# Three chunks per bank instead of two in the second MLP's output projection of tokens 256 to 1279, second half first, and output weights decoded a chunk later

## The chip, the cores and the metric

The kernel runs on one core of a Trainium2 chip. The metric is the device time of one execution in microseconds (us). Engines: PE multiplies matrices (PEld is its weight load, which overlaps), DVE is the vector engine, ACT the scalar engine, POOL the general-purpose engine, SP issues most DMAs.

## The reference

`attn_out` is an attention over a window of 64 positions (4 sequences of 576 tokens, 8 heads of 64). Its output is 2304 tokens by 512 features and goes through two gated MLPs with d_ff = 1536:

```python
def _moe_ref(x, w_gate, w_val, w_out):
    gate = 1.0 / (1.0 + np.exp(-(x @ w_gate)))
    return (gate * (x @ w_val)) @ w_out

def _moe2_ref(x, w_a, w_b, w_out):
    return ((x @ w_a) * (x @ w_b)) @ w_out

x = _moe_ref(attn_out as 2304 x 512, first weights)
return _moe2_ref(x, second weights)
```

The change touches the second MLP alone.

## The kernel before

**Chunks and split products.** d_ff is cut into 12 chunks of 128 columns. Each fp32 operand is a pair, a high and a low part in PE's own fp32 format, and each product is three matmuls (high by high, high by low, low by high). In the names, `wh`/`wl`, `xh`/`xl`, `hh`/`hl` are such parts.

**Weights.** The weights come as 64-bit words and are decoded on chip, matrix by matrix: a, b and o (the output matrix) of a chunk. For one matrix, `decode_words` (line 371) issues ACT L374 and L377, DVE L380 and L383, POOL L387; `decode_pair` (line 392) issues DVE L393, ACT L399 (the high part) and L402 (the low part, on DVE for a and b, on POOL for o), and `save` stores the pair to DRAM for later stages. Raw words arrive through three staging buffers `st`; when decoding of a matrix begins, the load of the same matrix of the next chunk is issued (`load_matrix`). The order of decoding is the list `order` (line 637): a, b, o of a chunk, then of the next. `step_decode` takes one step of it, `need(F)` takes steps until chunk F is `ready`. Decoded pairs lie in the pool `wts`, four buffers for each of a, b and o. F counts the chunks of both MLPs, so second-MLP chunk fc is F = 12 + fc. POOL and ACT also form sums of the chunk's a and b for the products below (`wq`, lines 439 to 442, called combinations here).

**The stage.** The change is in the stage that works on tokens 256 to 1279 with the second MLP, 343.6 to 592.25 us of the trace. These four blocks go through the first two products together, as a scheme of seven products per chunk (`quad`, matmuls at L846, in the order 1, 5, 6, 2, 7, 4, 3). PSUM results are kept or added by ACT L865 and DVE L868, DVE L878 multiplies a by b, and the result is two halves: h0, ready within the chunk, from pool `hp` (5 buffers for each part), and h1, ready at its end, in one of three places taken in turn (`seconds`: a buffer of its own, one of `wts` tag wa, one of tag wb). L470 writes a high part `hh`.

**The output projection.** `row_banks` (L1103) lists eight jobs for h0 and h1 of two chunks (PAIR = 2): four row blocks of h0, then four of h1. A job is `bank_sum` (L980): its matmuls (L984), three for each chunk, run into one PSUM bank `accq` (pool `ps_acc`, two buffers); then ACT L986 copies the bank to the sum `resf` (first pair), or DVE L988 adds it (all later ones). The jobs wait in a list `rest`; `fill(n)` issues n of them. `between(i)`, called after product i of a quad, issues some (a table `counts`) and takes one step of decoding. After each second quad what is left of `rest` is issued and the next eight jobs are listed.

**Block 0.** Tokens 0 to 255 are taken along: before quads 0, 2 and 4, `hidden` (L461 matmuls, L485, L470) computes two chunks of block 0 each ("the alone chunks"), and their projection (L514, added at L584 and L586) is one more job in `rest`.

**What sets the order.** A scheduler moves instructions within each engine's queue, so the order of the code is not the order on the engine; the excerpts in the section on the change show the orders that result. Each engine runs its own queue strictly in that order.

**What comes behind.** The last bank sums of this stage run beside `hidden` of chunks 9 to 11 of block 0; then the same seven products begin for another set of tokens, at 592.25 us.

Of the kernel before, what the change touches and what calls it, by code (L numbers as in the profile page):

```python
# [21 lines left out]
def tile_window_attention_gated_mlps(ctx, tc, q, k, v, w1g, w1v, w1o, w2a, w2b, w2o, out):  # L22
# [5 lines left out]
    NP = H // 2  # L28
    NF = DFF // P
    G = 3  # L30
    N = 256
# [337 lines left out]
    def decode_words(F, i, nm):  # L369
        st = staged.pop((F, nm))  # L370
        w0, w1 = st[:, :, 0], st[:, :, 1]
        k = 3 * F + i if F > NF + 2 else 0
        low = dec.tile([P, DM], I32, tag="low", name="low")
        nc.scalar.activation(out=low, in_=w0.bitcast(U32), func=AF.Copy, scale=2.0 ** -29)  # L374
        yield
        ex = late["dec"].tile([P, DM], F32, tag="ex", name="ex") if k % 3 == 2 else dec.tile([P, DM], F32, tag="ex", bufs=2, name="ex")
        nc.scalar.activation(out=ex, in_=w1.bitcast(F32), func=AF.Abs)  # L377
        yield
        wi = (late["dec"] if k % 2 else dec).tile([P, DM], I32, tag="wi", name="wi")
        nc.vector.tensor_scalar(  # L380
            out=wi, in0=w1, scalar1=3, scalar2=(1 << 30) - 1, op0=ALU.logical_shift_left, op1=ALU.bitwise_and
        )
        nc.vector.scalar_tensor_tensor(  # L383
            out=wi, in0=w1, scalar=-(1 << 30), in1=wi, op0=ALU.bitwise_and, op1=ALU.bitwise_or
        )
        yield
        nc.gpsimd.tensor_tensor(out=wi, in0=wi, in1=low, op=ALU.add)  # L387
        wordy[F, nm] = ex, wi
        yield
# [244 lines left out]
    NW = 2 * NF  # L634

    limit = [NF - 1]
    order = [(F, i, nm) for F in range(DECODED, NW) for i, nm in enumerate("abo")]
    held = [None]
    begun, pending, combined_by = [0], [], []

    def begin_matrix():
        if begun[0] == 0:
            load_weights(DECODED)
        if begun[0] < len(order):
            F, i, nm = m = order[begun[0]]
            begun[0] += 1
            since = len(nc.cur_bb.bb.instructions)
# [7 lines left out]
            pending.append(m)  # L655
            if F + 1 < NW:
                load_matrix(F + 1, nm)

    def step_decode(turn):
# [16 lines left out]
        save(F, nm, pairs.pop((F, nm)))  # L676
        if nm == "o":
            ready[F] = parts[F]
        elif nm == "b" and F >= NF:
            combined_by.append(combining(F))  # L680
        return True

# [7 lines left out]

    def need(F, turn):
        while F not in ready:
            assert step_decode(turn), (F, turn)
# [408 lines left out]

    def row_banks(res, hs, rows, begin, end):  # L1103


        banks = []
        for i in range(2 * NP):
            j, sl = i // NP, slice(i % NP * P, (i % NP + 1) * P)
# [17 lines left out]
    x_ops = next(built)  # L1126
    PAIR = 2
    NEVER = 1 << 30
# [10 lines left out]
    for fc in range(NF):  # L1139
        alone = ALONE.get(fc, ())  # L1140
        for i, f0 in enumerate(alone):
# [4 lines left out]
            if i == len(alone) - 1:  # L1146
                rest.append(lambda a=(1, 0, h0s, fc == 0, False): projection(*a))
                h0s = []
# [7 lines left out]
        g = [tmp.tile([P, W], F32, tag="hr", name=f"g{i}") for i in range(2)]  # L1156
        counts = ((0, 0, 1, 1, 1, 1, 0), (0, 0, 1, 1, 1, 1, 0)) if len(rest) <= 4 else ((0, 1, 1, 1, 1, 1, 1), (0, 1, 1, 1, 1, 1, 1))
        extra = max(0, len(rest) - sum(counts[0]))

        def between(i):  # L1160
            fill(counts[0][i] + (extra if i == 4 else 0))
            if i != 3:
                step_decode(NEVER)

        hs.append((w["o"], quad(1, w, x_ops, between, g, seconds[fc % 3], lambda: None)))
        if len(hs) == PAIR:
            fill(len(rest))
            row_banks(res, hs, (3 * N, N), fc == PAIR - 1, fc == NF - 1)
            hs = []
# [10 lines left out]
    h0s = []  # L1180
# [147 lines left out]
```

## Time and profile before

| | us |
|---|---|
| time, median of three runs | 965.94 |
| lowest and highest run | 965.51, 966.07 |
| profiled execution, its own time | 966.96 |
| span in that profile | 965.1 |
| PE busy | 927.0 (96%) |
| DVE busy | 705.4 (73%) |
| ACT busy | 480.0 (50%) |
| POOL busy | 358.7 (37%) |

The span runs from the first to the last instruction on the engines; 1.9 us of the profiled execution's time lie around it. PE is close to full over the whole span, so what can be gained or lost by another order of the same matmuls is PE's idle time, which has to be looked for stage by stage: a window's length less PE's busy time in it. In a timeline, the bracket behind an instruction names the idle time ahead of it and what ended it. The granted clock of PE is 1.00 in every window of the stage.

### The profile page before, as it was taken

To read this page: it belongs to the slowest core of one execution; us is meant where nothing else is said; L and a number is where in the kernel's file an instruction comes from. 1 tells how busy PE (TensorE), PEld (TensorE's weight loads), DVE (VectorE), ACT (ScalarE), POOL (GpSimd) and SP (SyncE) were. 2 spreads that over 40 slices of the span, in tenths; PEclk is the share of its full clock that TensorE was granted. 3 is DMA by queue.
4 is the path that set the end of the run, shared out by engine and by line. 5 is a ranking of instruction groups with operands and counts; after the bars stand their busy time and mean duration, and the time that the engine had idled before them with its cause. 6 is when DMAs were issued, how large, how long until landed. Compare 5 with 4: busy or idle time off the path is not lost.

```text
span 965.1 us, 15642 instructions
## 1 busy us (share of the span) xinstructions
PE 927.0 (96%) x5504; PEld 772.7 (80%) x5504; DVE 705.4 (73%) x1343; ACT 480.0 (50%) x1063; POOL 358.7 (37%) x357
## 2 busy tenths in 40 slices
PE   7899999999999988899999998999999999999998
PEld 6798888888887766787777886788888888888886
DVE  7997877876567899967979576778888673354545
ACT  7887555677635456564645334654454233211111
POOL 4443232343248738855758217644440000000000
PEclk9999999999999999999999999999999999999999
DMA  8987698997478637763765547345456675554312
GB/s 213 247 238 222 217 316 287 336 292 239 138 235 287 218 131 233 257 210 130 251 231 195 196 151 254 117 160 168 135 173 199 217 254 159 167 168 129 102 66 87
DMA packets 144684, 193.68 MB, mean 201 GB/s; under 512 B 63584, under 2 KB 98912, under 8 KB 143968
## 3 DMA queue, kind: packets, MB, share of 16 engines
q1 hardware_dynamic: 144608, 192.71, 61.6%
q8 instruction: 43, 0.70, 0.3%
q14 instruction: 33, 0.27, 0.1%
HBM read 118.75 MB, written 69.47 MB: 195 GB/s over the span
## 4 chain that ended last, share of the span: by engine, by line
PE 48%; DVE 9%; POOL 3%; DMA 3%; issue 2%; ACT 1%; DVEq 0%; POOLq 0%; ACTq 0%
PE qa L846 16%; PE accq L984 11%; PE qb L846 8%; PE qc L846 4%; PE accy L947 3%; PE accx L947 2%; DVE wi L380 1%; DMA st_a<-in_moe_w_a_dram 1%; DVE ex L393 1%; POOL s L439 1%; DVE wi L383 1%; POOL wq L442 1%; PE gps L461 1%; PE vps L461 1%; PE acc L514 1%
## 5 line engine op out<-in xcount | busy, mean ns | idle before, releaser
L387 POOL TENSOR_TENSOR wi<-wi,low 128x512 int32<-128x512 int32 x72 | 103.9, 1443 | 144.2 <-DVE wi L383 109.6
L865 ACT ACTIVATE r<-qa 128x512 f32<-128x512 f32 x108 | 63.6, 596 | 107.6 <-PE qa L846 93.6
L442 POOL TENSOR_TENSOR wq<-s,wq 128x256 fp32r<-128x256 f32 x96 | 86.5, 907 | 73.7 <-ACT wq L441 72.3
L846 PE MATMUL qa<-op,wq 128*128 128x512 f32 x432 | 112.9, 389 | 0.4 <-ACT r L865 0.4
L846 PE MATMUL qb<-op,wq 128*128 128x512 f32 x432 | 111.1, 389 | 0.9 <-DVE qc L868 0.9
L461 PE MATMUL gps<-xh,wa 128*128 128x256 f32 (+1 forms) x392 | 104.9, 338 | 1.5 <-DVE h L472 1.0
L461 PE MATMUL vps<-xh,wb 128*128 128x256 f32 (+1 forms) x392 | 105.3, 337 | 0.8 <-ACT hr L485 0.8
L846 PEld LDWEIGHTS qb<-op,wq 128*128 128x128 f32 x432 | 81.0, 188 | 18.1 <-DVE qc L868 1.3
L846 PEld LDWEIGHTS qa<-op,wq 128*128 128x128 f32 x432 | 80.9, 188 | 17.3 <-ACT r L865 0.6
L562 PE MATMUL accm<-hh,wo 128*128 128x512 f32 (+1 forms) x296 | 87.3, 362 | 3.3 <-DVE gacc L539 1.9
L461 PEld LDWEIGHTS gps<-xh,wa 128*128 128x128 f32 x392 | 68.6, 189 | 11.4 <-DVE h L472 1.5
L461 PEld LDWEIGHTS vps<-xh,wb 128*128 128x128 f32 x392 | 68.9, 189 | 8.7 <-ACT hr L485 1.0
L984 PE MATMUL accq<-wo,h 128*128 128x512 f32 (+1 forms) x300 | 71.7, 382 | 2.8 <-DVE resf L988 2.7
L393 DVE SCALAR_TENSOR_TENSOR ex<-ex,wi 128x512 f32<-128x512 f32 x72 | 59.7, 829 | 17.7 <-POOL wi L387 10.3
L984 PEld LDWEIGHTS accq<-wo,h 128*128 128x128 f32 x300 | 54.9, 188 | 14.9 <-DVE resf L988 3.8
L461 PE MATMUL gps<-xl,wa 128*128 128x256 f32 (+1 forms) x196 | 65.6, 335 | 0.6 <-DVE xl L237 0.6
L470 ACT ACTIVATE hh<-qa 128x512 fp32r<-128x512 f32 x36 | 21.6, 599 | 89.0 <-DVE qa L878 60.0
L461 PE MATMUL vps<-xl,wb 128*128 128x256 f32 (+1 forms) x196 | 65.6, 335 | 0.0
L562 PEld LDWEIGHTS accm<-hh,wo 128*128 128x128 f32 x296 | 54.1, 193 | 13.8 <-DVE gacc L539 4.4
L984 PE MATMUL accq<-wo,hh 128*128 128x512 f32 x184 | 55.7, 394 | 4.9 <-ACT hh L470 3.7
L846 PE MATMUL qa<-op,wa 128*128 128x512 f32 x216 | 55.7, 391 | 3.3 <-DVE g L868 3.3
L846 PE MATMUL qa<-op,wb 128*128 128x512 f32 x216 | 55.3, 391 | 2.4 <-ACT r L865 2.4
(177 smaller groups left out, 2114.9 us busy)
## 6 DMA issues: line engine op xcount, KB each, us to landing
wo<-ko SPq DMA_DIRECT2D x27, 512.0 KB, 3.9
wa<-ka SPq DMA_DIRECT2D x27, 512.0 KB, 4.6
st_o<-in_moe_w_out_dram SPq DMA_DIRECT2D x24, 512.0 KB, 4.9
ka<-wa SPq DMA_DIRECT2D x24, 512.0 KB, 5.1
kb<-wb SPq DMA_DIRECT2D x24, 512.0 KB, 4.1
ko<-wo SPq DMA_DIRECT2D x24, 512.0 KB, 4.0
kq<-wq SPq DMA_DIRECT2D x48, 256.0 KB, 3.2
wq<-kq SPq DMA_DIRECT2D x48, 256.0 KB, 3.2
```

Of the source, the lines that this page charges most:

```text
L380: nc.vector.tensor_scalar(out=wi, in0=w1, scalar1=3, scalar2=(1 << 30) - 1, op0=ALU.logical_shift_left, op1=ALU.bitwise_and)
L383: nc.vector.scalar_tensor_tensor(out=wi, in0=w1, scalar=-(1 << 30), in1=wi, op0=ALU.bitwise_and, op1=ALU.bitwise_or)
L387: nc.gpsimd.tensor_tensor(out=wi, in0=wi, in1=low, op=ALU.add)
L393: nc.vector.scalar_tensor_tensor(out=wf, in0=wf, scalar=SMALLEST, in1=wi.bitcast(F32), op0=ALU.is_ge, op1=ALU.mult)
L442: nc.gpsimd.tensor_tensor(out=t[:, 1], in0=s, in1=t[:, 0].bitcast(F32), op=ALU.subtract)
L461: nc.tensor.matmul(ps, lhsT=a[:, c * P:(c + 1) * P], rhs=b[:, c, :], start=(n == 0), stop=(n == 3 * NP - 1))
L470: nc.scalar.activation(out=hh, in_=hr, func=AF.Copy, scale=factor)
L562: nc.tensor.matmul(ps[:, m], lhsT=a[:, sl], rhs=b, start=k == 0, stop=k == total - 1)
L846: nc.tensor.matmul(ps, lhsT=a[:, c * P:(c + 1) * P], rhs=b[:, c, :], start=first and n == 0, stop=n == 5, skip_group_check=True,)
L865: nc.scalar.activation(out=r[n], in_=ps, func=AF.Copy)
L947: nc.tensor.matmul(bank[k], lhsT=a[n][i][:, sl], rhs=b[n][j], start=start and m == 0, stop=m == 2, skip_group_check=True,)
L984: nc.tensor.matmul(ps, lhsT=a, rhs=b, start=n == 0, stop=n == len(pairs) - 1)
```

## The change

**Banks over three chunks.** `THREE = 3` takes the place of `PAIR`: eight jobs are listed after quads 2, 5, 8 and 11, each of nine matmuls instead of six. That is 32 jobs in place of 48 (the very last one is split in two by columns, as before). The number of matmuls is the same. In the first three quads there is no bank sum to issue; before, there was none in the first two.

**Second half first.** `turned=True` lists the four h1 jobs ahead of the four h0 jobs.

**Order of decoding.** Above F = 14, `order` has a and b of a chunk ahead of o of the chunk before; o of the last chunk comes last. A chunk is ready when its b is there and its combinations are formed; `need(..., "o")` stands ahead of a projection and of a list of banks. Loads follow `order`, three matrices ahead, and the buffers `ex` and `wi` are chosen by the place in `order`.

**Issue.** `counts` becomes (0, 1, 1, 0, 1, 1, 0) for every quad, four jobs; what four a quad don't take of `rest` (`extra`) is issued in the third quad after a list, behind product 4.

Everything else is the same, line numbers of the changed kernel apart (L846 is L851 there, L868 L873, L878 L883, L984 L989, L986 L991, L988 L993, L755 L760, L758 L763).

```diff
 def decode_words(F, i, nm):
-        k = 3 * F + i if F > NF + 2 else 0
+        k = order.index((F, i, nm)) if F > NF + 2 else 0
...
-    order = [(F, i, nm) for F in range(DECODED, NW) for i, nm in enumerate("abo")]
+    order = [(F, i, nm) for F in range(DECODED, NF + 2) for i, nm in enumerate("abo")]
+    for F in range(NF + 2, NW):
+        order += [(F, 0, "a"), (F, 1, "b")] + ([(F - 1, 2, "o")] if F > NF + 2 else [])
+    order.append((NW - 1, 2, "o"))
...
-            if F + 1 < NW:
-                load_matrix(F + 1, nm)
+            if at + 3 < len(order):
+                load_matrix(*order[at + 3][::2])
...
-        if nm == "o":
+        if nm == "o" and F < NF:
             ready[F] = parts[F]
         elif nm == "b" and F >= NF:
             combined_by.append(combining(F))
+            ready[F] = parts[F]
...
-    def need(F, turn):
-        while F not in ready:
+    def need(F, turn, nm="b"):
+        while F not in ready or nm not in parts[F] or nm == "b" and combined_by:
...
-    def row_banks(res, hs, rows, begin, end):
+    def row_banks(res, hs, rows, begin, end, turned=False):
-        for i in range(2 * NP):
+        for i in (*range(NP, 2 * NP), *range(NP)) if turned else range(2 * NP):
...
-                rest.append(lambda a=(1, 0, h0s, fc == 0, False): projection(*a))
+                def projected(a=(1, 0, h0s, fc == 0, False), last=NF + f0):
+                    need(last, NEVER, "o")
+                    projection(*a)
+
+                rest.append(projected)
...
-        counts = ((0, 0, 1, 1, 1, 1, 0), (0, 0, 1, 1, 1, 1, 0)) if len(rest) <= 4 else ((0, 1, 1, 1, 1, 1, 1), (0, 1, 1, 1, 1, 1, 1))
-        extra = max(0, len(rest) - sum(counts[0]))
+        counts = (0, 1, 1, 0, 1, 1, 0)
+        extra = max(0, len(rest) - sum(counts)) if len(hs) == THREE - 1 else 0
...
-        if len(hs) == PAIR:
+        if len(hs) == THREE:
             fill(len(rest))
-            row_banks(res, hs, (3 * N, N), fc == PAIR - 1, fc == NF - 1)
+            need(NF + fc, NEVER, "o")
+            row_banks(res, [(w["o"], h) for w, h in hs], (3 * N, N), fc == THREE - 1, fc == NF - 1, True)
```

PE's queue in quads 1 and 2, before. `qa`, `qb`, `qc` are PSUM banks of the seven products, `op` and `wq` their token and weight operands, `x6` six matmuls in a row:

```order
L846 MATMUL qa_4995<-op7_4762,wq7_4421 128x512 x6
L846 MATMUL qc_5229<-op2_4617,wa_4866 128x512 x6
L846 MATMUL qa_4995<-op4_4766,wb_4370 128x512 x6
L846 MATMUL qb_4996<-op3_4768,wq3_4427 128x512 x6
L846 MATMUL qa_5227<-op6_4725,wq6_4924 128x512 x6
L984 MATMUL accq_5160<-wo_4442,hh_5097 128x512 x2
L984 MATMUL accq_5168<-wo_4442,hh_5097 128x512 x2
```

The same place in the changed kernel:

```order
L851 MATMUL qa_4980<-op7_4762,wq7_4380 128x512 x6
L851 MATMUL qc_5182<-op2_4616,wa_4866 128x512 x6
L851 MATMUL qa_4980<-op4_4766,wb_4362 128x512 x6
L851 MATMUL qb_4981<-op3_4768,wq3_4386 128x512 x6
L851 MATMUL qa_5180<-op6_4725,wq6_4924 128x512 x6
L461 MATMUL gps_5112<-xh1_0_4728,wa_4866 128x256
```

The bank sums of the first pair, which stood here, are gone from this place; the alone chunks' `hidden` comes next.

DVE's queue at the start of the stage, before (`ex`, `wi`: decoding; `xl1`, `op4`: token operands):

```order
L393 SCALAR_TENSOR_TENSOR ex_4857<-ex_4857,wi_4859 128x512
L571 TENSOR_TENSOR xl1_0_4729<-gacc0_1020,xh1_0_4728 128x512 x2
L380 TENSOR_SCALAR wi_4880<-st_o_4439 128x512
L755 TENSOR_TENSOR op4_4766<-gacc30_2076,op4_4766 128x1024
L402 TENSOR_TENSOR wb_4887<-ex_4857,wb_4887 128x512
L383 SCALAR_TENSOR_TENSOR wi_4880<-st_o_4439,wi_4880 128x512
```

And in the changed kernel:

```order
L393 SCALAR_TENSOR_TENSOR ex_4857<-ex_4857,wi_4859 128x512
L571 TENSOR_TENSOR xl1_0_4729<-gacc0_1020,xh1_0_4728 128x512 x2
L393 SCALAR_TENSOR_TENSOR ex_4895<-ex_4895,wi_4897 128x512
L380 TENSOR_SCALAR wi_4995<-st_b_4446 128x512
L760 TENSOR_TENSOR op4_4766<-gacc30_2076,op4_4766 128x1024
L402 TENSOR_TENSOR wb_4904<-ex_4857,wb_4904 128x512
L383 SCALAR_TENSOR_TENSOR wi_4995<-st_b_4446,wi_4995 128x512
```

The o matrix that was decoded here (`st_o`) has given its place to the next chunk's b (`st_b`), with its L393 a step earlier.

ACT's queue where the first list of banks ends, before:

```order
L377 ACTIVATE ex_5517<-st_a_5389 128x512
L986 ACTIVATE resf3_4841<-accq_5317 128x512
L377 ACTIVATE ex_5654<-st_b_5428 128x512
L399 ACTIVATE wo_5392<-ex_5269 128x512
L986 ACTIVATE resf3_4841<-accq_5334 128x512
L399 ACTIVATE wa_5663<-ex_5517 128x512
L377 ACTIVATE ex_5443<-st_o_5275 128x512
```

And in the changed kernel:

```order
L470 ACTIVATE hh_5535<-vps_5519 128x256
L485 ACTIVATE hr_5587<-gps_5561 128x256
L991 ACTIVATE resf1_4839<-accq_5594 128x512
L470 ACTIVATE hh_5590<-vps_5574 128x256
L399 ACTIVATE wo_5491<-ex_5375 128x512
L399 ACTIVATE wo_5700<-ex_5652 128x512
L991 ACTIVATE resf1_4839<-accq_5605 128x512
L377 ACTIVATE ex_5781<-st_b_5637 128x512
```

Two o matrices (`wo_5491`, `wo_5700`) and an `hh` of the alone chunks now stand between the copies of the list's last two banks (`accq_5594`, `accq_5605`), ahead of the further decoding.

## Rows read from the trace of the kernel before

**Rows 1.** The page, busy time of each engine over the whole span

```profile
PE 927.0 (96%) x5504; PEld 772.7 (80%) x5504; DVE 705.4 (73%) x1343; ACT 480.0 (50%) x1063; POOL 358.7 (37%) x357
```

**Rows 2.** Busy time by stretch: stretch, its length, busy time (instructions), clock, DMA

```profile
376.00:416.00 40.00, 33.69 (x165) 26.83 (x164) 35.73 (x45) 24.24 (x48) 29.95 (x26) 1.00 0.61 211
416.00:440.00 24.00, 24.00 (x119) 20.29 (x118) 20.50 (x27) 15.82 (x31) 18.25 (x18) 1.00 0.80 272
440.00:480.00 40.00, 36.67 (x171) 30.03 (x170) 33.90 (x51) 18.67 (x38) 25.20 (x24) 1.00 0.54 189
480.00:530.00 50.00, 47.78 (x210) 38.92 (x209) 43.77 (x64) 27.11 (x51) 34.44 (x35) 1.00 0.60 208
530.00:568.00 38.00, 37.94 (x172) 31.06 (x171) 22.74 (x34) 13.52 (x23) 5.88 (x7) 1.00 0.38 139
568.00:592.00 24.00, 20.44 (x121) 17.53 (x121) 18.24 (x25) 7.83 (x17) 16.32 (x17) 1.00 0.73 244
```

**Rows 3.** Timeline of PE: start, duration, matmuls, [idle before, what ended it]

```profile
382.18 1.65 PE L846 MATMUL qa<-op,wa 128*128 128x512 f32 x6 [1.72 <-DVE g L868]
...
396.59 1.20 PE L984 MATMUL accq<-wo,hh 128*128 128x512 f32 x4 [1.11 <-ACT hh L470]
...
445.70 0.73 PE L984 MATMUL accq<-wo,hh 128*128 128x512 f32 x2 [1.05 <-DVE resf L988]
...
477.60 1.19 PE L984 MATMUL accq<-wo,hh 128*128 128x512 f32 x4 [1.24 <-ACT hh L470]
...
526.66 1.65 PE L846 MATMUL qa<-op,wa 128*128 128x512 f32 x6 [1.54 <-DVE g L868]
...
582.85 2.36 PE L984 MATMUL accq<-wo,h 128*128 128x512 f32 x12 [1.73 <-DVE resf L988]
...
588.72 0.73 PE L514 MATMUL acc<-wo,hh 128*128 128x512 f32 x2 [1.49 <-DVE resf L988]
```

**Rows 4.** Timeline of DVE: last product of quads 0, 1, 2 and 8

```profile
383.57 0.69 DVE L878 TENSOR_TENSOR qc<-qc,g 128x512 f32<-128x512 f32 x1
...
398.43 0.68 DVE L878 TENSOR_TENSOR qc<-qc,g 128x512 f32<-128x512 f32 x1
...
416.80 0.70 DVE L878 TENSOR_TENSOR qc<-qc,g 128x512 f32<-128x512 f32 x1
...
527.73 0.68 DVE L878 TENSOR_TENSOR qc<-qc,g 128x512 f32<-128x512 f32 x1
```

**Rows 5.** Timeline of PE: places in the stage, twelve matmuls, the next stage

```profile
416.10 1.52 PE L846 MATMUL qa<-op,wq 128*128 128x512 f32 x6
...
458.98 2.88 PE L984 MATMUL accq<-wo,h 128*128 128x512 f32 x12
...
461.70 0.39 PE L846 MATMUL qa<-op,wq 128*128 128x512 f32 x1
...
592.25 1.52 PE L846 MATMUL qa<-op,wa 128*128 128x512 f32 x6
```

**Rows 6.** Groups by line and shape, DVE, 376 to 536 us

```profile
L393 DVE SCALAR_TENSOR_TENSOR ex<-ex,wi 128x512 f32<-128x512 f32 x26 | 25.8, 993 | 2.5 <-ACT ex L377 1.4 <-POOL wi L387 1.0
...
L988 DVE TENSOR_TENSOR resf<-accq,resf 128x512 f32<-128x512 f32 x24 | 16.0, 682 | 6.1 <-PE accq L984 6.1
```

**Rows 7.** Groups by line and shape, whole run

```profile
L986 ACT ACTIVATE resf<-accq 128x512 f32<-128x512 f32 x8 | 4.5, 594 | 1.0 <-PE accq L984 1.0
...
L402 POOL TENSOR_TENSOR wo<-ex,wo 128x512 fp32r<-128x512 f32 x12 | 17.3, 1441 | 11.1 <-ACT wo L399 9.0 <-PE accq L984 1.8
...
L399 ACT ACTIVATE wo<-ex 128x512 fp32r<-128x512 f32 x24 | 15.1, 630 | 7.6 <-DVE ex L393 5.2 <-PE accm L562 1.2 <-PE accq L984 0.8
```

**Rows 8.** Waits of POOL, 376 to 592 us: total, times, longest

```profile
POOL wo L402 <- ACT wo L399: 7.0, 5, 2.8
```

**Rows 9.** Timeline of DVE near the stage's end

```profile
580.82 1.38 DVE L802 TENSOR_TENSOR t<-xq,t 128x1024 f32<-128x1024 f32 x1
...
582.12 1.27 DVE L988 TENSOR_TENSOR resf<-accq,resf 128x512 f32<-128x512 f32 x2
```

More of the change, by code (lines that the diff above doesn't have):

```diff
@@ L645, in begin_matrix @@
             F, i, nm = m = order[begun[0]]
+            at = begun[0]
             begun[0] += 1
@@ L1126, in tile_window_attention_gated_mlps @@
     x_ops = next(built)
-    PAIR = 2
+    PAIR, THREE = 2, 3
     NEVER = 1 << 30
@@ L1156, in tile_window_attention_gated_mlps @@
         g = [tmp.tile([P, W], F32, tag="hr", name=f"g{i}") for i in range(2)]
-        counts = ((0, 0, 1, 1, 1, 1, 0), (0, 0, 1, 1, 1, 1, 0)) if len(rest) <= 4 else ((0, 1, 1, 1, 1, 1, 1), (0, 1, 1, 1, 1, 1, 1))
-        extra = max(0, len(rest) - sum(counts[0]))
+        counts = (0, 1, 1, 0, 1, 1, 0)
+        extra = max(0, len(rest) - sum(counts)) if len(hs) == THREE - 1 else 0
         def between(i):
-            fill(counts[0][i] + (extra if i == 4 else 0))
+            fill(counts[i] + (extra if i == 4 else 0))
             if i != 3:
                 step_decode(NEVER)
-        hs.append((w["o"], quad(1, w, x_ops, between, g, seconds[fc % 3], lambda: None)))
-        if len(hs) == PAIR:
+        hs.append((w, quad(1, w, x_ops, between, g, seconds[fc % 3], lambda: None)))
+        if len(hs) == THREE:
             fill(len(rest))
-            row_banks(res, hs, (3 * N, N), fc == PAIR - 1, fc == NF - 1)
+            need(NF + fc, NEVER, "o")
+            row_banks(res, [(w["o"], h) for w, h in hs], (3 * N, N), fc == THREE - 1, fc == NF - 1, True)
             hs = []
```

## The prediction

> **What bounds the kernel now.** I read the busy times first [rows 1]: PE works 96% of the span, DVE 73%, ACT and POOL about half or less. The change neither adds nor removes a matmul, so it can move the time only through PE's idle time, and only in its own stage. The busy times by stretch give that idle time as length less PE's busy time [rows 2]: 6.31 us in 376 to 416, 0 in 416 to 440, 3.33 in 440 to 480, 2.22 in 480 to 530, 0.06 in 530 to 568 and 3.56 in 568 to 592, in all 15.48 us. The clock is 1.00 in each stretch, so it plays no part. The same rows show who fills the time: DVE is busy 35.73 of 40 us in the first stretch and 98.2 of 114 us from 416 to 530, while ACT has room everywhere. DMA is busy 0.38 to 0.80 of the time and leaves room too.
>
> Then the timeline of PE says what ends each gap [rows 3]. Early: 1.72 us for the quad's g at L868 and 1.11 for an `hh` at L470. In the middle (440 to 530): 1.05 for `resf`, that is for a PSUM bank to be added up by DVE, 1.24 for an `hh`, 1.54 for g; with two of 1.04 and 0.67 us that I don't show, five gaps make the 5.54 us of these two stretches. In the tail (568 to 592): 1.73 and 1.49 for `resf`, which is DVE taking 1.27 us for two adds [rows 9] while both buffers of `ps_acc` are full. Nearly all of these are waits for DVE, at once or one step removed, so the question is how much DVE work stands beside how much PE work in each third of the stage.
>
> **Early part, quad 0 to quad 2.** DVE's products at L878 end quads 0, 1 and 2 at 383.57, 398.43 and 416.80 us [rows 4]. Between the first two DVE is never idle: 18 instructions in 14.86 us, 0.83 us each. In the order from quad 0's product to quad 2's DVE has 37 instructions before and 40 after (the excerpts show one cause: o of a chunk gives way to the next chunk's b, whose L393 and low part are DVE's; o's low part is POOL's). Three more are 2.5 us. PE loses its filler there: the first pair's banks, 12 matmuls in these quads by the order, go behind quad 2. Twelve matmuls take 461.70 − 458.98 = 2.72 us [rows 5], 0.227 each. So at worst the early gaps grow by 2.5 + 2.7 = 5.2 us. But nothing is lost if DVE goes at its full rate throughout: 40 instructions, of which four are of half size, make 38 × 0.83 = 31.5 us, so quad 2's product would start at 415.1, not later than the 416.80 of before, where DVE had some 4 us of waits in the second half. The first bank needs quad 2's h1 and could start some 1.2 us behind, at about 416.3. Summing PE's order at 0.227 a matmul from the stage's start, its first bank stands behind 55.8 us of work in the changed kernel, and just as much work was behind PE at 416.10 before [rows 5]. Hence the lower bound is 0, the upper 5.2. I take **+1.0**: near the lower end, since DVE's measured rate decides, but not at it, as DVE will not be without any wait.
>
> **Middle, quad 2 to quad 8.** From 416.80 to 527.73 us [rows 4] DVE has 135 instructions before and 119 after. Twelve are adds of banks, since a list of three chunks has eight adds, not twelve: two take 1.27 us [rows 9], so 12 × 0.64 = 7.6 us (0.68 each by the group's mean [rows 6], 8.2). Four are steps of decoding, which has run on more before or after: 4 × 0.99 [rows 6] = 4.0 us. So 11.6 us of DVE work leave a stretch of 110.9 us in which PE idles 5.54.
>
> Against it stands a new wait. Three output matrices are held till the list's last bank has read them, and `wo` has four buffers. The excerpt of ACT shows the consequence: `wo_5491` and `wo_5700` stand ahead of the copy of the last bank `accq_5605`, and an `hh` of the alone chunks ahead of them. ACT's queue is in order, so decoding, the combinations behind it on POOL and the quad's r copies wait with them. By the sum over PE's order the alone product that gives this `hh` ends at 81.3 us of PE work and the last bank at 84.0 or so: at most 2.7 us per list, and for three lists 8.1 us. Before, POOL's waits for `wo` were 7.0 us in five times, the longest 2.8 [rows 8], so such a hand-over is no new size; the operations themselves take 0.6 us (the copy of a bank, L399) and 1.4 us (L402 on POOL) [rows 7]. Net 11.6 − 8.1 = 3.5 us less in the way of PE: of 5.54 us, 2.0 stay. **−3.5**; the bounds are −5.5, if the hand-overs lie beside PE's work, and a loss, which is the third rival.
>
> **Tail.** From the last quad's end to the next stage at 592.25 [rows 5] PE has 22.9 us of matmuls before and 27.8 after, at the same nine adds and the same operands on DVE (one of these is 1.38 us, as [rows 9] shows). A bank takes 9 × 0.227 = 2.04 us instead of 1.36, so with two buffers PE covers 1.36 us more of DVE's absence: 1.73 becomes 0.37, a gap of 0.34 us that I don't show becomes 0, and 1.49, which stands ahead of the projection of block 0 and not of a bank, stays. 2.07 − 0.37 = **−1.7**. Lower bound −3.0 (all but a rest of the 3.56 us), upper 0 (the banks come later, into the same DVE work).
>
> **At nothing.** The turned order: h1 lies in a `wa` and a `wb` buffer, and their early release lets decoding of a and b go on, work that is counted above. Loads three matrices ahead in the new order: there are still three `st` buffers and as many loads, and DMA is busy 0.54 to 0.61 in the crowded stretches [rows 2]; uncovered, one load late would be one such wait of up to 2.8 us [rows 8]. The saves and the next stage's fetches come no later relative to that stage.
>
> **Sum.** +1.0 − 3.5 − 1.7 = −4.2 us on a profiled execution of 966.96 us: 962.8. The median of the runs is 965.94, 1.0 lower, so the forecast is 965.94 − 4.2 = **961.7 us**. Its own range lets the early part go from 0 to +3 and the middle from −5.0 to −2.5: −6.7 to −1.2 us, 959.2 to 964.7, say 959 to 964.5.
>
> **First rival: the gain is whole.** If decoding two chunks ahead keeps DVE's peaks away from the quads' ends, all 5.54 us of the middle go, 3.0 of the tail, and the early part gains 1.0: 9.5 us, 956.4. For it: 11.6 us of freed DVE work are twice the gaps. Against it: `hh` gaps (1.11, 1.24) [rows 3] are ACT's queue, which the change does not empty. 0.14.
>
> **Second rival: no change.** The early part costs its full 5.2 us, since for three quads PE has no bank to turn to when a product waits for DVE, as it turns to at 396.59 and 445.70 now [rows 3]; −3.5 − 1.7 give it back: 0.0, 965.9. For it: 35.73 of 40 us of DVE are taken there [rows 2], and three more instructions have to be placed. By the order two banks of the second list also stay open for 17.7 us of PE work, where before the longest was 9.3, and with both buffers open PE has no third bank to go to. The Trainium skill, page "PSUM — Partial Sum Buffer", section "Summary: rules for kernel authors", speaks against holding banks: it advises to evacuate promptly, since PSUM is small. The trace agrees in so far as gaps of 1.05 to 1.73 us end with a bank's addition [rows 3]. By that rule the middle would gain nothing, and the sum would be +1.0 − 1.7 = −0.7, 965.2. 0.18.
>
> **Third rival: slower, by the hand-over of `wo`.** If the matrices at the end of a list arrive while half of its banks are yet to run, ACT stands for 4 × 2.04 = 8.2 us at each hand-over, and decoding and r copies with it. Two such hand-overs before decoding ends are 16.3 us; less the 11.6 freed this is 4.7 us more idle time in the middle. +1.0 + 4.7 − 1.7 = +4.0: 969.9. It decides from about 6.1 us a hand-over on: 2 × 6.1 − 11.6 = 0.7, which with +1.0 takes up the tail's gain. For it: a list's buffer count (three held of four) leaves one matrix of slack where before two were left. Against it: longest measured wait of this kind 2.8 us [rows 8], and the order puts `wo` just ahead of the last bank, not of the fifth. 0.21.
>
> **How the numbers follow.** Forecast 0.47, rivals 0.14, 0.18 and 0.21. About 0.2%, 1.9 us, is what a measurement of this kernel can tell from no change. The forecast's own range and the first rival lie below that: faster 0.61. The second lies within: 0.18. The third lies above: 0.21. For 8 in 10 the range takes in the forecast, the second rival, and the larger part of the first and third: 956.5 to 969.9.
>
> **What would show it.** Right: in the timeline of PE the first three quads keep gaps of 6 to 8 us in all in what was 376 to 416; the stretch from quad 2 to quad 8 has about 2 us of them; one `resf` gap in the tail is nearly gone; the group of bank adds counts a third fewer instructions; the waits of ACT's `wo` for PE's banks stay under 3 us each. Wrong: waits of `wo` of 6 us or more (third rival), early gaps of 11 us (second), or gaps at places that have none now, such as 416 to 440 or 530 to 568.

## The result and the profile after

The changed kernel takes 972.73 us (median of four runs, 971.49 to 973.64) against 966.01 for the kernel before on the same chip: a ratio of 1.0070, 95% interval 1.0055 to 1.0085. It is slower by 6.7 us where 4.2 us less was forecast. A second set of runs on another chip gave 972.0 against 966.38, 1.0056 (1.0030 to 1.0081).

The page of the changed kernel, busy time of each engine (the answer to [rows 1]); its span is 971.7 us:

```profile
PE 936.1 (96%) x5507; PEld 780.8 (80%) x5507; DVE 692.4 (71%) x1327; ACT 478.0 (49%) x1063; POOL 354.5 (36%) x357
```

PE is idle for 971.7 − 936.1 = 35.6 us, where it was 965.1 − 927.0 = 38.1. So in these two executions it waits 2.5 us **less** than before, but the same matmuls keep it busy 9.1 us **longer**. The sum of the two is the 6.6 us by which the spans differ. The work is the same: three matmuls of 512 columns have become six of 256 (5507 records in place of 5504), since the last bank, which is split in two by columns, has nine matmuls now and not six. What differs is the granted clock, the third column from the end in the same windows as [rows 2]:

```profile
376.00:416.00 40.00, 35.84 (x169) 29.76 (x168) 34.04 (x48) 24.05 (x49) 31.97 (x30) 0.91 0.64 224
416.00:440.00 24.00, 24.00 (x119) 20.37 (x118) 17.87 (x26) 13.82 (x29) 14.81 (x15) 1.00 0.64 220
440.00:480.00 40.00, 37.24 (x168) 30.61 (x167) 30.23 (x43) 23.28 (x45) 26.77 (x25) 0.96 0.56 198
480.00:530.00 50.00, 45.77 (x194) 37.05 (x194) 41.45 (x57) 25.92 (x49) 34.52 (x34) 0.97 0.63 227
530.00:568.00 38.00, 37.20 (x165) 29.87 (x164) 19.29 (x30) 12.21 (x20) 5.25 (x5) 1.00 0.39 131
568.00:600.00 32.00, 29.75 (x161) 25.14 (x160) 20.29 (x28) 8.97 (x18) 16.43 (x19) 0.95 0.64 208
```

In [rows 2] the clock is 1.00 in all six; here it is 0.91, 0.96, 0.97 and 0.95 in four. (The stage starts at 343.96 us here, 0.33 later than before. The clock is also low between 11 and 18 us in this profile, and between 11 and 16 us in the second profile of the changed kernel; the change does not touch that part, which makes PE busy 1.2 us longer in the first 50 us.)

[Rows 2] begins at 376 us, and the stage at 343.6. In its first part the clock fell in the kernel before too, behind two waits close together, so it is not 1.00 in every window of the stage. The window, the two waits, and four microseconds behind them:

```profile
343.00:376.00 33.00, 28.39 (x148) 24.09 (x147) 30.98 (x40) 20.31 (x38) 18.58 (x16) 0.95 0.44 151
```

```profile
350.12 0.50 PE L562 MATMUL accm<-hh,wo 128*128 128x256 f32 x2 [1.23 <-ACT hh L470]
352.68 0.58 PE L562 MATMUL accm<-hl,wo 128*128 128x256 f32 x1 [2.05 <-DVE hl L472]
```

```profile
352.00:356.00 4.00, 3.33 (x15) 3.33 (x16) 4.00 (x6) 1.09 (x2) 1.50 (x1) 0.58 0.10 21
```

In the changed kernel the same window, with waits of 1.23 and 2.06 us in it, has a clock of 0.90.

The timeline of PE from 376 us on, the waits that are over 0.4 us, and the start of the next stage (to be read against [rows 3] and [rows 5]):

```profile
388.56 1.78 PE L851 MATMUL qa<-op,wb 128*128 128x512 f32 x6 [2.45 <-ACT r L870]
...
392.05 2.93 PE L851 MATMUL qb<-op,wq 128*128 128x512 f32 x6 [1.71 <-DVE qc L873]
...
474.24 2.07 PE L851 MATMUL qa<-op,wa 128*128 128x512 f32 x6 [2.76 <-DVE g L873]
...
525.55 2.17 PE L851 MATMUL qa<-op,wa 128*128 128x512 f32 x6 [4.20 <-DVE g L873]
...
566.99 0.39 PE L461 MATMUL gps<-xh,wa 128*128 128x256 f32 x1 [0.79 <-DVE hl L472]
...
594.52 1.05 PE L514 MATMUL acc<-wo,hh 128*128 128x512 f32 x2 [1.79 <-DVE resf L993]
...
599.64 1.52 PE L851 MATMUL qa<-op,wa 128*128 128x512 f32 x6
```

Before there were, from 376 us on, a dozen waits of at most 1.73 us; now there are six that matter, and they are longer. Windows of four microseconds show what the clock does behind three of them:

```profile
388.00:392.00 4.00, 1.78 (x6) 1.05 (x6) 3.99 (x5) 0.81 (x3) 3.89 (x4) 0.74 0.77 280
392.00:396.00 4.00, 3.95 (x9) 3.17 (x10) 2.77 (x5) 2.75 (x6) 3.26 (x3) 0.50 0.55 221
472.00:476.00 4.00, 1.76 (x6) 1.50 (x7) 3.98 (x6) 2.74 (x6) 3.92 (x5) 0.91 0.14 54
476.00:480.00 4.00, 4.00 (x13) 3.14 (x13) 2.44 (x5) 2.85 (x6) 1.67 (x3) 0.66 0.42 137
524.00:528.00 4.00, 2.45 (x8) 1.93 (x9) 4.00 (x6) 2.87 (x7) 3.29 (x6) 0.81 0.32 132
528.00:532.00 4.00, 4.00 (x15) 3.25 (x14) 3.73 (x6) 1.72 (x5) 2.74 (x4) 0.76 0.36 138
```

0.50 is the lower of the clock's two levels, 1.2 GHz: six matmuls at 392.05 take 2.93 us, where six take 1.52 to 1.65 elsewhere. Such a stretch at the lower level is called a fall of the clock in what follows. Each fall takes away 1.7 us of full clock (0.09 × 4 + 0.34 × 4 behind 474.24), the pair of waits at 388 to 392 about twice that.

The 9.1 us are those of one pair of profiles, and these two lie near the two ends: the mean clock over the whole span is 0.997 in the profiled execution before and 0.983 in this one. Over all executions it is 0.995 on average for the kernel before (the 84 executions beside the experiments) and 0.989 for the changed kernel (eleven). The difference, 0.006 of some 970 us, is 5.8 us of full clock, about as much as the kernel is slower; this is an estimate, since a low clock costs nothing while PE waits. The second profile of the changed kernel lies between: PE is busy 932.9 us and idle 35.1.

**Where the long waits come from.** The wait at 525.55 can be followed operation by operation. DVE's queue in the changed kernel, ahead of it:

```profile
520.10 0.85 DVE L380 TENSOR_SCALAR wi<-st_o 128x512 int32<-128x512 int32 x1
520.98 1.64 DVE L383 SCALAR_TENSOR_TENSOR wi<-st_o,wi 128x512 int32<-128x512 int32 x1
522.55 0.68 DVE L402 TENSOR_TENSOR wa<-ex,wa 128x512 fp32r<-128x512 f32 x1
523.15 0.69 DVE L883 TENSOR_TENSOR qa<-qa,g 128x512 f32<-128x512 f32 x1
523.75 1.15 DVE L393 SCALAR_TENSOR_TENSOR ex<-ex,wi 128x512 f32<-128x512 f32 x1
524.82 0.68 DVE L873 TENSOR_TENSOR g<-qb,r 128x512 f32<-128x512 f32 x1
```

and in the kernel before, at the same quad:

```profile
522.15 0.41 DVE L380 TENSOR_SCALAR wi<-st_o 128x512 int32<-128x512 int32 x1
522.48 0.69 DVE L878 TENSOR_TENSOR qa<-qa,g 128x512 f32<-128x512 f32 x1
523.08 1.18 DVE L402 TENSOR_TENSOR wa<-ex,wa 128x512 fp32r<-128x512 f32 x1
524.18 1.22 DVE L383 SCALAR_TENSOR_TENSOR wi<-st_o,wi 128x512 int32<-128x512 int32 x1
525.33 0.68 DVE L393 SCALAR_TENSOR_TENSOR ex<-ex,wi 128x512 f32<-128x512 f32 x1
525.93 0.68 DVE L868 TENSOR_TENSOR g<-qb,r 128x512 f32<-128x512 f32 x1
```

It is the same work: four operations of decoding around the quad's own, then the g that PE waits for. What differs is PE's side. Before, two banks stood in PE's queue ahead of that wait:

```profile
522.01 1.52 PE L984 MATMUL accq<-wo,h 128*128 128x512 f32 x6
523.37 0.39 PE L846 MATMUL qa<-op,wq 128*128 128x512 f32 x1
523.60 1.52 PE L984 MATMUL accq<-wo,h 128*128 128x512 f32 x6
```

Twelve matmuls, 2.72 us, and the wait of 1.54 at 526.66 behind them [rows 3]: 4.26 us together. In the changed kernel nothing stands there, and the wait is 4.20. A list of three chunks is used up by the second quad after it, so the third quad has no bank left when DVE finishes it.

(On names: PE's queue runs ahead of the quad that DVE finishes, and quads take two sets of PSUM banks in turn. The waits at 474.24 and 525.55 stand at the ends of quads 5 and 8, the third quads of a list, and ahead of product 1 of quads 7 and 10, which needs these quads' banks. They are called the waits at quads 7 and 10 below.)

### The profile page after: what moved, and what is told of

The parts are those of the page before. It is cut to its first block, busy times and chain, and to the rows that moved or that the text cites. A ratio compares the mean times of both kernels' runs of the same rounds, so it can differ in the third digit from the quotient of the medians.

```text
span 971.7 us, 15632 instructions
## 1 busy us (share of the span) xinstructions
PE 936.1 (96%) x5507; PEld 780.8 (80%) x5507; DVE 692.4 (71%) x1327; ACT 478.0 (49%) x1063; POOL 354.5 (36%) x357
## 4 chain that ended last, share of the span: by engine, by line
PE 52%; DVE 6%; POOL 3%; issue 2%; ACT 2%; DMA 1%; ACTq 0%; DVEq 0%; POOLq 0%
PE qa L851 18%; PE accq L989 12%; PE qb L851 9%; PE qc L851 4%; PE accy L952 3%; PE accx L952 2%; PE acc L514 1%; PE gps L461 1%; PE vps L461 1%; POOL wq L442 1%; POOL s L439 1%; POOL wi L387 1%; DVE ex L393 1%; DMA ks<-opair 1%; DVE op L800 1%
## 5 line engine op out<-in xcount | busy, mean ns | idle before, releaser
L851 PE MATMUL qa<-op,wq 128*128 128x512 f32 x432 | 115.1, 398 | 0.3 <-ACT r L870 0.3
L851 PE MATMUL qb<-op,wq 128*128 128x512 f32 x432 | 113.3, 397 | 2.0 <-DVE qc L873 1.7
L442 POOL TENSOR_TENSOR wq<-s,wq 128x256 fp32r<-128x256 f32 x96 | 83.9, 878 | 79.5 <-ACT wq L441 74.9
L851 PEld LDWEIGHTS qb<-op,wq 128*128 128x128 f32 x432 | 82.7, 192 | 20.9 <-DVE qc L873 2.7
L851 PEld LDWEIGHTS qa<-op,wq 128*128 128x128 f32 x432 | 83.4, 194 | 18.6 <-ACT r L870 1.0
L393 DVE SCALAR_TENSOR_TENSOR ex<-ex,wi 128x512 f32<-128x512 f32 x72 | 58.8, 818 | 20.6 <-ACT ex L377 10.4
L989 PE MATMUL accq<-wo,h 128*128 128x512 f32 (+1 forms) x303 | 71.9, 380 | 0.1
L470 ACT ACTIVATE hh<-qa 128x512 fp32r<-128x512 f32 x36 | 21.5, 598 | 95.0 <-DVE qa L883 66.1
L851 PE MATMUL qa<-op,wa 128*128 128x512 f32 x216 | 56.6, 396 | 8.2 <-DVE g L873 7.0
L989 PEld LDWEIGHTS accq<-wo,h 128*128 128x128 f32 x303 | 54.9, 188 | 11.4 <-DVE h L472 0.4
L851 PE MATMUL qa<-op,wb 128*128 128x512 f32 x216 | 55.6, 392 | 4.1 <-ACT r L870 4.1
L189 ACT ACTIVATE pr<-pr,stat 128x128 f32<-128x128 f32 x144 | 54.1, 392 | 7.5 <-DVE stat L183 7.4
```

What stands on the lines that cost most here:

```text
L189: nc.scalar.activation(out=pr[e][:, j, :], in_=pr[e][:, j, :], func=AF.Exp, bias=nmax[:, e, j:j + 1], scale=-1.0, accum_out=None if t in O ...
L393: nc.vector.scalar_tensor_tensor(out=wf, in0=wf, scalar=SMALLEST, in1=wi.bitcast(F32), op0=ALU.is_ge, op1=ALU.mult)
L442: nc.gpsimd.tensor_tensor(out=t[:, 1], in0=s, in1=t[:, 0].bitcast(F32), op=ALU.subtract)
L470: nc.scalar.activation(out=hh, in_=hr, func=AF.Copy, scale=factor)
L851: nc.tensor.matmul(ps, lhsT=a[:, c * P:(c + 1) * P], rhs=b[:, c, :], start=first and n == 0, stop=n == 5, skip_group_check=True,)
L989: nc.tensor.matmul(ps, lhsT=a, rhs=b, start=n == 0, stop=n == len(pairs) - 1)
```

## The experiments

Two theories of the loss. **The clock:** PE's waits are fewer, but the longer ones take its clock down, and the slow matmuls behind them are what costs. **The chain:** DVE and ACT set the pace at the ends of the quads, and the clock merely follows. And two of where the long waits come from: **1a**, no bank is at hand at the end of a list's third quad; **1b**, the new decode order puts decoding ahead of the quad's additions in DVE's queue. Ratios are to the kernel before on the same chip.

### Filling the waits with matmuls that compute nothing

```diff
+    TABLE = {(1, 4): (2, 2), (1, 3): (2, 1), (7, 1): (6, 3), (10, 1): (9, 4)}
+    for (q, n), (of, times) in TABLE.items():
+        at = next(j for j, i in enumerate(listed) if i.name == firsts[q, n])
+        listed[at:at] = emit(of, times)
```

Each entry puts, ahead of quad q's product n, so many matmuls of zeros into PE's finished queue, added to the open bank of quad `of`; nothing else moves, and no engine waits for them.

> The changed kernel with its order untouched and ten matmuls added that compute nothing new (zeros, fp32, 128x512, added to a bank that is open anyway): two ahead of quad 1's product 4, one ahead of its product 3, three ahead of quad 7's product 1, four ahead of quad 10's product 1. These are the places of PE's four longest waits in the stage (2.45, 1.71, 2.76 and 4.20 us), behind which the granted clock fell. Theory 1 (the clock): PE waits less than before in all, 35.6 us instead of 38.1, but its matmuls take 9.1 us longer, since a long wait takes the clock down behind it; without these waits the three falls of about 3.4, 1.7 and 1.7 us go: 972.7 - 6.8 = 966, although PE has some 9 us more work. Theory 2 (the chain): DVE and ACT decide when the products go on, and the clock only follows; then added matmuls cannot help: 972.7 or more.

Measured: 968.12 us against 967.16, ratio 1.0003 (0.9986 to 1.0020). The twenty records of added matmuls, two for each, are 9.2 us of PE's time. The timeline of PE at quad 7 and the windows at the four places:

```profile
471.60 2.73 PE L851 MATMUL qb<-start,ident 128*128 128x512 f32 x6
474.52 1.65 PE L851 MATMUL qa<-op,wa 128*128 128x512 f32 x6 [0.19 <-DVE g L883]
```

```profile
386.00:400.00 14.00, 12.28 (x59) 9.04 (x58) 13.02 (x17) 9.18 (x19) 13.14 (x12) 1.00 0.66 236
470.00:482.00 12.00, 11.81 (x47) 8.45 (x46) 11.06 (x15) 7.03 (x15) 10.31 (x11) 1.00 0.51 179
520.00:534.00 14.00, 13.20 (x52) 9.27 (x51) 13.47 (x18) 7.13 (x14) 10.76 (x11) 1.00 0.56 220
590.00:602.00 12.00, 10.21 (x46) 8.11 (x45) 8.92 (x11) 4.25 (x8) 4.28 (x5) 1.00 0.65 224
```

With 9.2 us more to do the span is 967.9 us against 971.7, and the clock is 1.00 at all four places. PE is busy 937.9 us; less the added matmuls that is 928.7 for the kernel's own, which took 936.1 in the changed kernel's profile.

> The changed kernel with four added matmuls of 0.92 us in place of ten: one ahead of quad 1's product 4, one ahead of quad 7's product 1, two ahead of quad 10's. The waits should go from 2.45, 2.76 and 4.20 us to 1.5, 1.8 and 2.4. The clock theory: two of the three falls go, 967 to 969 where the changed kernel has 972 and the full fill had 0.03% over the kernel before; with no fall left it is as good as the full fill. If matmuls cost here what they cost elsewhere: 972 + 3.7 = 976.

```diff
+    TABLE = {(1, 4): (2, 1), (7, 1): (6, 1), (10, 1): (9, 2)}
```

Measured: 972.58 against 966.92, ratio 1.0052 (1.0036 to 1.0067): no gain. The waits shrank as expected, to 1.60, 1.90 and 2.51 us (and 1.83 ahead of quad 1's product 3, which had no filler), but the clock fell all the same. The same four windows:

```profile
386.00:400.00 14.00, 10.58 (x49) 8.55 (x49) 12.48 (x16) 8.00 (x16) 12.51 (x12) 0.88 0.60 209
470.00:482.00 12.00, 10.10 (x36) 7.52 (x36) 10.39 (x17) 7.62 (x15) 8.43 (x10) 0.86 0.50 178
520.00:534.00 14.00, 11.49 (x40) 8.32 (x39) 12.37 (x17) 6.50 (x13) 9.87 (x11) 0.88 0.48 191
590.00:602.00 12.00, 9.82 (x36) 7.34 (x35) 8.27 (x11) 3.35 (x5) 3.29 (x3) 0.86 0.58 203
```

My expectation of two falls fewer was wrong. But the pair decides between the theories: the full fill has 5.5 us more useless work than the half fill and still stands 0.0049 lower in ratio, 4.7 us. The order of all real instructions is the same in both, so what differs is the clock: the deficit (one minus the clock, times the window) is 6.7 us in these four windows of the half fill and nothing in those of the full one. It is not only these two executions: the mean clock of the ten runs each is 0.996 with the full fill and 0.991 with the half fill. The chain theory falls, as it wanted 972.7 or more for the full fill.

> The changed kernel once more, on the chip of the three runs beside it. The clock theory: the same four or five waits of over 1.7 us, but not each of them takes the clock down in each execution, so the executions lie apart by one or two falls of 1.7 us: about 969 to 974, median 971 to 973. If the waits themselves cost the time, the executions agree within 1 us.

Measured: 968.32 to 975.56 us in seven runs, median 972.0, as expected. That the executions lie apart by the number of their falls is not shown, however. Six of the seven have the same mean clock, 0.989, and take from 970.1 to 975.56 us; the 23 runs of the kernel before beside them spread from 963.26 to 969.19, with little regard to their clocks of 0.993 to 0.998. What spreads the single executions stays open.

### Which part of the change makes the waits

> The changed kernel with the decode order of before (a, b, o of each chunk); three chunks per bank, the turned order and the issue counts stay. Theory 1a (no bank at hand): PE's long waits come because a list of three chunks has no job left at the end of its third quad; the waits at quads 7 and 10 stay near 2.8 and 4.2 us and the time near 972. Theory 1b (decoding in DVE's queue): they come because the new order puts L380, L383 and L393 of decoding ahead of the quad's additions; the waits fall under 2 us and the time comes to about 967.

```diff
-    order = [(F, i, nm) for F in range(DECODED, NF + 2) for i, nm in enumerate("abo")]
-    for F in range(NF + 2, NW):
-        order += [(F, 0, "a"), (F, 1, "b")] + ([(F - 1, 2, "o")] if F > NF + 2 else [])
-    order.append((NW - 1, 2, "o"))
+    order = [(F, i, nm) for F in range(DECODED, NW) for i, nm in enumerate("abo")]
```

Measured: 978.59, ratio 1.0127 (1.0089 to 1.0164), worse than both theories said. Quad 7's wait stays at 2.81 us, which is against 1b; quad 10's, which 1a wanted near 4.2, is not to be seen. There are new ones, the first behind a weight sum of POOL's, the second behind an ACT copy:

```profile
522.41 1.19 PE L848 MATMUL qb<-op,wq 128*128 128x512 f32 x4 [1.72 <-POOL wq L442]
...
567.85 1.76 PE L848 MATMUL qa<-op,wb 128*128 128x512 f32 x6 [3.10 <-ACT r L867]
```

POOL's waits in this kernel bear on the first:

```profile
POOL wo L402 <- ACT wo L399: 43.1, 5, 21.1
```

One of the five, 14.49 us long, ends at 505.57 us, 17 us ahead of PE's first new wait, and the sums queued on POOL come behind it. The ACT operation that it waits for had itself waited 2.06 us for a bank sum. That is the third rival's hand-over, but at 2.06 us (and 3.20 at a second place) where that rival has 8.2; that PE's wait follows from it is argued, not shown. The second wait is another matter: the copy stands in ACT's queue behind L796, which waited 2.80 us for a load of the next stage's operand. PE is idle 4.7 us longer than in the changed kernel's profile (976.8 − 936.5 = 40.3 us) and busy as long, so what this kernel loses beyond that one is waiting. In the changed kernel ACT's part of `wo` never waits over 1.1 us for a bank in either profile; that the new decode order, which puts o behind the next a and b, is what keeps the hand-over harmless there fits these two runs, the only difference between the kernels being that order.

> Two chunks per bank, first half first and the issue counts of before, with the new decode order alone. Theory 1a: no long wait, clock as before, 965 to 967. Theory 1b: long waits at the ends of the quads and a clock under 0.99, 969 to 973.

```diff
-    PAIR, THREE = 2, 3
+    PAIR, THREE = 2, 2
...
-        counts = (0, 1, 1, 0, 1, 1, 0)
-        extra = max(0, len(rest) - sum(counts)) if len(hs) == THREE - 1 else 0
+        counts = (0, 0, 1, 1, 1, 1, 0) if len(rest) <= 4 else (0, 1, 1, 1, 1, 1, 1)
+        extra = max(0, len(rest) - sum(counts))
...
-            row_banks(..., fc == THREE - 1, fc == NF - 1, True)
+            row_banks(..., fc == THREE - 1, fc == NF - 1)
```

Measured: 965.43 against 967.16, ratio 0.9982 (0.9968 to 0.9997): a small gain. Of the parts of the change, the decode order by itself helps a little. Ahead of quads 7 and 10 there is no wait over 0.6 us, so 1b falls there. The one long wait, 2.67 us, is in quad 1, where the kernel before waits 1.02 and 0.88; there 1b may hold.

> The changed kernel with h0's banks ahead of h1's, as before; three chunks per bank, the new decode order and the new counts stay. By the order four and two bank matmuls now stand beside quad 7's product 1 and four and two beside quad 10's, where none stood. Theory 1a (no bank at hand there): the waits of 2.8 and 4.2 us shrink by 1.4 each and one or two falls of the clock go, 968 to 970. Rival (h1 has three places in all, and they are held until the list's end): quads 3, 6 and 9 wait for their h1 at their ends, 973 to 978.

```diff
-            row_banks(..., fc == THREE - 1, fc == NF - 1, True)
+            row_banks(..., fc == THREE - 1, fc == NF - 1)
```

Measured: 973.5, ratio 1.0074 (1.0049 to 1.0099). The banks that now stand at quads 7 and 10 wait themselves, for an `hh` (2.37 and 2.24 us, both ended by ACT L470): h0 of the list's third quad is the one thing that they need and that DVE and ACT have not finished. No wait for h1 at the ends of quads 3, 6 and 9 shows, so the rival's time came without its mechanism.

> The changed kernel with counts (0, 0, 1, 1, 1, 1, 0): one job of a quad is issued a product or two later. By the order quad 8's end gets five bank matmuls between product 7 and product 2 of the next quad in place of six elsewhere; the places ahead of quads 7 and 10 hold no bank in it either. Theory 1a: both waits stay, 971 to 973. Theory 1b: the same; a time under 969 would be against both.

```diff
-        counts = (0, 1, 1, 0, 1, 1, 0)
+        counts = (0, 0, 1, 1, 1, 1, 0)
```

Measured: 971.01, ratio 1.0040 (1.0020 to 1.0060), in ten runs from 967.31 to 975.04. Both waits stay, at 2.77 and 4.21 us. The profiled execution happens to be a quick one, and one row of it is instructive. The timeline and a window at quad 7:

```profile
471.22 1.66 PE L851 MATMUL qa<-op,wa 128*128 128x512 f32 x6 [2.77 <-DVE g L873]
```

```profile
466.00:478.00 12.00, 9.23 (x41) 7.29 (x40) 10.85 (x14) 7.55 (x15) 10.28 (x12) 1.00 0.47 172
```

The same wait as in the changed kernel, 2.77 against 2.76 us, and no fall of the clock behind it: six matmuls take 1.66 us there and 2.07 here. The wait opens the possibility; whether the clock falls is not settled by its length. (These are one execution each of two kernels, which differ in where one bank of a quad is issued.)

> The changed kernel with the eight jobs of a list spread over three quads (3, 3, 2) in place of two (4, 4). By the order quad 7's product 1 still has no bank ahead of it, but the third quad of a list has 9 to 18 bank matmuls more in its first half, 2.0 to 4.1 us. Theory 1a: DVE gets this much more time at the third quad, and the waits at quads 7 and 10 go from 2.8 and 4.2 us to under 1.7; quad 1's stays: clock 0.993 or more, 965 to 969. Rival (the output matrices and h0 are held until the list's last bank, and decoding stands behind it): new waits for POOL's or ACT's part of wo, 972 to 976.

```diff
-        counts = (0, 1, 1, 0, 1, 1, 0)
+        counts = ((0, 1, 1, 0, 1, 0, 0), (0, 1, 1, 0, 1, 0, 0), (0, 0, 1, 0, 1, 0, 0))[len(hs)]
```

Measured: 969.66 against 966.38, ratio 1.0037 (1.0022 to 1.0052). The waits at quad 1 (2.43), quad 7 (2.97) and near quad 10 (2.56) are still there, so the expectation missed. My explanation, which no run isolates, is that PE work in the first half of the third quad moves the quad's products and DVE's chain behind them alike. Matmuls just ahead of the wait do cover it, as the full fill shows (2.76 us became 0.19), and there a list of three has none that is ready, as the run with the first half first showed. 1a stands in this narrower form.

### Can the useful part be kept

> Two chunks per bank with the new decode order, as in e2_decode_order_alone, and four added matmuls that compute nothing new (zeros, fp32, added to an open bank): one ahead of quad 1's product 4, three ahead of its product 3, where PE waited 1.23 and 2.67 us and the clock fell behind. The clock theory: the fall of 1.7 us goes, 963.5 to 964.5 where e2 had 965.4. If the clock is not what costs: 965.4 or more.

The kernel with the decode order alone, and added matmuls in quad 1:

```diff
+    TABLE = {(1, 4): (2, 1), (1, 3): (2, 3)}
```

Measured: 964.29 against 966.38, ratio 0.9979 (0.9966 to 0.9993). By ratio that is no more than the 0.9982 without the fill, so this run does not tell a single fall of the clock from the intervals.

> Two chunks per bank as before, with the new decode order from one chunk later on (the first two chunks of it are decoded a, b, o). In e2_decode_order_alone the one long wait of the stage, 2.67 us, came in quad 1, where the next chunk's b stood in DVE's queue in place of o. If that is its cause, the wait falls under 1.7 us as before and the clock stays: about 964, 0.2 to 0.3% under the kernel before. If it comes from elsewhere: 965.4 as in e2.

Against the kernel with the decode order alone:

```diff
-    order = [(F, i, nm) for F in range(DECODED, NF + 2) for i, nm in enumerate("abo")]
-    for F in range(NF + 2, NW):
-        order += [(F, 0, "a"), (F, 1, "b")] + ([(F - 1, 2, "o")] if F > NF + 2 else [])
+    order = [(F, i, nm) for F in range(DECODED, NF + 3) for i, nm in enumerate("abo")]
+    for F in range(NF + 3, NW):
+        order += [(F, 0, "a"), (F, 1, "b")] + ([(F - 1, 2, "o")] if F > NF + 3 else [])
```

Measured: 965.97, ratio 0.9991 (0.9976 to 1.0006). Quad 1 waits 2.69 and 2.08 us here, so the place of that one b in DVE's queue was not the cause of that wait; the expectation missed.

> The same, with the new decode order from two chunks later on. As e10_decode_order_later or a little nearer to the kernel before, 964 to 966; without a long wait in the stage if the clock theory is to hold for a time under 965.

Measured (the same edit with 4 in place of 3): 963.22 against 966.92, ratio 0.9963 (0.9947 to 0.9980), 3.6 us under the kernel before and the best of the study. Its windows from 440 to 530 us:

```profile
440.00:480.00 40.00, 40.00 (x193) 33.55 (x192) 36.63 (x53) 21.05 (x41) 27.94 (x26) 1.00 0.61 207
480.00:530.00 50.00, 48.01 (x209) 38.50 (x208) 43.29 (x67) 26.48 (x52) 32.21 (x34) 1.00 0.62 224
```

PE's idle time there is 1.99 us, where [rows 2] gives 5.55; with the order changed from the first chunk or one later on it is 2.59 and 2.29. That is the 3.5 us that I had forecast for the middle, but by luck: it comes from the decode order alone, with all 48 jobs, and I had counted it mostly from the bank additions that larger lists save. The falls in the first stretch remain (quad 1's waits are 1.04, 1.28 and, ahead of quad 2's product 2, 2.11 us), so this part of the expectation, no long wait, did not hold. The three intervals, 0.9963, 0.9982 and 0.9991 with some 0.0015 to either side, do not tell the three starts of the new order from each other with certainty.

> e10b_decode_order_two_later (two chunks per bank, new decode order from two chunks later) with four added matmuls of 0.92 us that compute nothing new, where that kernel's profile shows its last three waits of the stage with a fall of the clock behind them: two ahead of quad 2's product 2 (2.11 us), one ahead of quad 1's product 4 (1.04), one ahead of its product 3 (1.28). The profile had about ten microseconds at 1.2 GHz there. The clock theory: that fall goes, about 2 us under e10b's ratio of 0.9963: 0.994 to 0.995. If added matmuls only cost: 0.9963 or more.

Against the kernel before this one:

```diff
+    TABLE = {(2, 2): (2, 2), (1, 4): (2, 1), (1, 3): (2, 1)}
```

Measured: 964.6 against 966.19, ratio 0.9988 (0.9979 to 0.9998). The clock stays up at these places in the profiled execution, which took 962.44 us, but the median is not better than without the fill; the expectation missed. The mean clocks suggest why the fill pays in the changed kernel and not here. There it went from 0.989 to 0.996, some 7 us of full clock. Here it went from 0.995 (six runs) to 0.996 (eleven), about 1 us, against 3.7 us of added matmuls: the profile that I filled by had a clock of 0.991, the lowest of its six runs, so an average run had less to be saved.

## Why the prediction was wrong

**The step that failed is the one sentence on the clock.** I read 1.00 in every stretch [rows 2] and concluded that the clock plays no part, so a microsecond of waiting counted the same in a wait of 1 us and in one of 4. In the profile before, no wait in the stage past 376 us is over 1.73 us [rows 3] and none has a fall behind it. After the change there are waits of 2.45, 2.76 and 4.20, with falls that make up most of the 9.1 us by which the matmuls are longer over the span. By idle time alone the forecast had the sign right: 2.5 and 3.0 us less in the two profiles, where I said 4.2 (slower matmuls may hide some of the waiting). The trace of the kernel before held the warning, 20 us ahead of where my table begins: waits of 1.23 and 2.05 us with a clock of 0.58 behind them. The Trainium skill, page "TensorE: Matmul & The Clock Gate", section "HAM oscillation — how this bites in real kernels", says that pauses of PE bring its clock down in the middle of a kernel; the windows at 0.50 and 0.66 agree. The pauses that the page describes are longer than most of the waits here; by the measurement, shorter ones do it too. I had not weighed that rule.

**Early part, +1.0.** The bounds were 0 to 5.2 us. The waits from 376 to 416 us sum to 4.16 instead of 6.31, so by idle time this window gained 2.2, of which the one ahead of it, 343 to 376, gave back 1.0 (5.62 us of waiting instead of 4.61). It was not DVE's rate that did it: from quad 0's last product to quad 2's (380.56 to 415.87 us) its 40 instructions took 35.3 us, where the lower bound had 31.5, but quad 0 ended 3.0 us earlier than before. And two long waits remained of many short ones, and about 3.4 us of clock were lost behind them.

**Middle, −3.5.** DVE's work did fall, and by the kind of amount that I counted: the group of bank adds over the same stretch as [rows 6] has 10 instructions where 24 were.

```profile
L993 DVE TENSOR_TENSOR resf<-accq,resf 128x512 f32<-128x512 f32 x10 | 6.7, 684 | 6.0 <-PE accq L989 6.0
```

Yet PE's idle time between 440 and 530 us went from 5.55 to 6.99, so this term, too, had the wrong sign: work that leaves DVE in one place does not shorten the chain at a quad's end in another. I compared sums over 110 us, and the wait is decided in five: that a list of three leaves the third quad without a bank was in the order, and I had looked at it for the first three quads only. The second rival has that mechanism for the early part; it recurs at quads 7 and 10.

**The wo hand-over, 8.1 of those 11.6 us.** POOL does stand much longer for `wo` than in [rows 8]:

```profile
POOL wo L402 <- ACT wo L399: 35.6, 4, 21.8
```

but none of PE's waits over 0.4 us is for POOL. That a and b of the next chunk were decoded ahead fits it. The term was charged against the wrong engine. The third rival's number, 969.9, is the nearest to the time, but its mechanism showed only with the old decode order, and smaller there.

**Tail, −1.7.** Right: 3.56 us became 0.40 and 1.79, −1.4. The fall behind the 1.79 then took about as much, in this execution; the second profile has none behind 1.78. A wait of 0.79 us at 566.99, in a stretch that had none, is new.

**What stays open.** Why one execution loses the clock behind a wait of 2.76 us and another keeps it behind 2.77; the price in time of a single fall, which the runs with one of them do not resolve; what in the decoding makes the waits at quad 1; and what spreads the executions of one kernel at the same mean clock.

## What to carry to other kernels

Where PE is nearly full, look at the length of its longest waits and not only at their sum: a change that makes a dozen short waits into four long ones can lose by the clock what it gains in idle time. Read the clock from the first window of a stage to its last before saying that it plays no part, and over more than one execution. Here, work that PE can always do, such as output sums, was worth more as filler at the ends of dependent chains than the additions that larger batches saved; before enlarging a batch, list for each long chain what stands in PE's queue beside it. And take a change apart: here one of its parts, the decode order from some chunks on, gave 0.37% alone (0.20 to 0.53).

## What was not expected of the hardware

Single waits of 1.79 and 1.90 us were followed by falls of the clock (the half-filled kernel), and so were 1.23 and 2.05 us close together (the kernel before, at 350 us), while waits of 1.54 to 1.73 us before [rows 3] and of 2.77 us in one execution were not. Adding 9.2 us of matmuls on zeros to the changed kernel brought its ratio from 1.0070 (1.0056 on the second chip) to 1.0003.
